# Three loads of batch 3 issued from earlier places in GpSimd's order

## The chip, the cores and the metric

One core of a Trainium2 chip runs the whole kernel. The time is device microseconds of one execution, lower is better.

## The reference

Attention with a feature map, then a two-layer network over the result. For each of 8 batches with 8 heads, 576 positions and 64 features:

```
phi(x) = [exp(p), exp(-p)],  p = x @ w_phi - max|x @ w_phi|      # w_phi: 64 x 128
kv  = phi(k)^T v,   z = sum over positions of phi(k)
x   = (phi(q) kv) / (phi(q) z + 1e-6)                            # 4608 tokens x 512
g   = elu(x @ w_in),   out = g @ w_out                           # w_in: 512 x 2048, w_out: 2048 x 512
```

q, k, v and the weights come in as float32 and are cast to bfloat16 while they are loaded.

## The kernel before

**Tiles.** The attention goes over 16 groups of four heads, n = 0 to 15; batch b is groups 2b and 2b + 1, so batch 3 is groups 6 and 7. The network goes over 9 chunks of 512 tokens; chunk 1 needs the attention of groups 2 and 3 (batch 1). From batch 1 on, `load` (L213) brings the whole of one batch's k, q or v (576 KB as bfloat16) with one DMA that GpSimd issues (L216). The pool `io` has two buffers for each of k, q and v, so batch 3 takes those of batch 1.

**From a load to its use.** k and q are needed transposed. For groups 0 to 3 TensorE transposes them (`t_pe`, L234); from group 4 on a DMA transpose that SyncE issues does it (`t_dma`, L252: L266 for k and for q of groups 4 and 5, two issues at L261 for q from group 6 on). `k_mm` (L294) and `m_mm` (L368 for groups up to 5, L353 from 6 on) are the first uses of kT and qT. v is multiplied on GpSimd by a weight for each position (`v_scale`, L331) ahead of the product with phi(k) (`kv_mm`, L516). The attention's result xp is transposed by SyncE too, into xT of its chunk (`x_dma`, L656) and into the last chunk (L663). SyncE also issues the stores of the output (L716).

**The network.** For each chunk and each of 16 tiles of hidden features: `h_mm` on TensorE (L672), the exponential on ScalarE (L683), the minimum with 1 on GpSimd (`h_min`, L688), the elu on VectorE (L692); then `o_mm` (L700). The first chunk goes in halves of 256 tokens.

**The order.** Each engine takes its instructions in the order in which the program emits them, and waits where an operand or a buffer isn't there. That order is written out by hand in the string ORDER (L18): each letter is a step (a star or a digit behind it chooses a variant or a PSUM bank), and each occurrence of a letter takes the next entry of the step's list. White space in the string means nothing. The letters that the change and the prediction touch:

```
e=(load, k)  f=(load, q)  g=(load, v)       # GpSimd issues; e and f, g begin with parts of batch 0
E=(v_scale)  F=(v_ones)   r=(h_min)         # GpSimd work
n=(t_dma, k) o=(t_dma, q) z=(x_dma) v=(o_store)   # SyncE issues
A=(k_mm) M=(m_mm) p=(h_mm) t=(o_mm)         # TensorE
q=(h_exp)  s=(h_elu)                        # ScalarE, VectorE
```

Of the kernel before, what the change touches and what calls it, by code (L numbers as in the profile page):

```python
# [19 lines left out]
DFFUV*M2NW6XBBP5Q*M0S4TTM2NNEU6j1kEEUV*j0k*OP2QS4TTM1NW6Xl0S2l1Y4ZTTj5km*mY7ZOP6Q*W3XS0TTp7A5Cp2  # L20
qrqrM3NS0TTissBp4qrj7kA0p3p2CsBqql6mrsrM4Nsp7p3BBM0Nqqp6p2DqqrrrA4BensssO*Cp0qY7Z*p3qp1qrsrrssrs
EW6XBl2m*p0p4qM2qrsrP1p5Q*DqES6TNM0NsS2TTTM0NFErsEFY6Zp7qrO*sA0BBA2BU4UVp7qp6CP5Q*qBt4S0Tforrss
p7qp5CTrsqp6qW2XW0p7ttXDqS2TA0ngrsErsrsEp5p6p7qrtTCp2qFqrrBsp3qqrp5u*BsqssrsrsDFp4qp7qrsErsS0TT
S2TTt6ttA0zzU4CoEUVA2CBBtuBBW4W0p7t6vzXXzzzzM2NA4DqBenvzftrsM0NM2Np7qrstA0BBBCDM2Ntu*O*P7Q*Ct5S2
TTtM6S0TTEEFNtM6NEFU3S0ogEUVA6CtW3TTBBDEp1p0p2XW6Xuqrqqp5qp3p4p7p6srsA0nerrfqqrsssqrsBBM2NqO*rr
p5p4p2qrCsqssDrqp1qp7P3Q*qsp6p5rrssErsFqA2BBM0NCEqp4rrssqrsFt7S0TtS2M5TTTNvvzzzzS0oTTtA5CEU2US0t
Vu*BBDFETTwW2XW4Xvt6A0BBCS2Ttttu*S0M4TTA2CDTFt7ttM0NBBA4BBM2NNCEEEgfDFEEztU0UV*A2CDzzp6qBup5qrr
W0xRt4tBp7qEEressoM0M2p6qrtNNW0xp5qsstu*S2M0p7p6TTrsRNqwp4qqrsS2TTyW0xrrssyp5p7qrqrS2TTnnA0CRp6q
vvzossp4qFU2UV*rsrsBBA5CDzvyzzW2xRp7qp4W0xp3p2rsyBBqrqzqS5TA0nCrrREyzzTssswDBBt7ttS3TTM5NEEEtu*
t2W3xRyA0BBS5ToTtttuCM3NM0NS5TTFFt7U3UA5A0tV*CCDBBDwBBW3xttuA2Czzp4qp5qBBW0xEEEfep7qrFFrrgssst6t  # L30
M1NS3TTtp7qRRM0NM3Np5p2nevvqrsyW0xqrrssEp3p7p4tS0oqrqqrrsssU2UVy*zzRyvzzuvS5TTTTp4qrW1xRp3qp5qrr
ssA0CS6TTp2qp4rDqp3W6qErrssxBBp5qrt2S0oA6BnssRByEtA3sttTTyzCDECFFW5xRyzzBBuvt7tM0A4BBM2NNttM0CED
ENU2UV*wS4TTt6W0W2ttA4nu*vzxxBBM0p7W2tFERqNuCDyxt1p5qA2BBgrsM6Np4qp0wqEECrsU6FfUV*M2NwtRy*A5CS2T
Tp7rsrRy*qtS2ovtsrsBBDETTgp4qrW5xRyp0uvp7qqS2TTsW5xp1qrp4rssqrrssA5nzzzzW2xRCp0qrp7p1p4p3qqqrrss
BBqp2qsyzrsErrFt7S0M5NttDFEETTssS0TToA5CM3Ntt2RyA0CBBBBU3UVM5NtzzzuvW3xRDtS5A0nCtFyEW3t7tTTBxRBD
wA5BBS3TTM0u*Ntp2qCW0xtuM5NFEEyzEU3UVM0NS5TovvrsRp7p3qqrsrsA0CTp4qp2p7qqByrrsp6qp3rqBrrssW4xssp2
qrst7A0BBS4Tp6p3p2ttqrqCqrrsssRyTDFEM0NA5BBM3NCtDuvp2qrsp1qrFt7EW3xp0qp2RyrqrzzzzEM3S5TTttsNssW3
xRyA5BBA0BCCwwDEFEEtut2tS3TTDEEU5UttV*Bt3W4S6S0ttxRy*u*TTTTW6xW4Rtt2xS0TTFU6Uy*Vzzp4p1u*qqrrsW5
p0p7qrssxqrp4p3p1p0qqrqRyssRrrW5xRp7tttsqrszy*y*W3xsp1p5qqrrp6p4p3vzzvqrvzzzzu*vRysszp2zqqrqrrsq
p7sqsrssrst1tttu*vt5tttt7ttuvp4p2p5p3qrtp0uvsqrqsrsqrqrssp4qp1p7t5tp6p0p2ttqqrrrsssp3p4qrqsrsuqq  # L40
qp7p1qrrrssrssp5qrqp2p0qp7rsrqrssp4sqrst1tttuqrst7tttt0tttuvu*vp1qp5p2rqrqrsssp4p7qrsqp1p2p0p5qq
rrqsst7tttuqp1p7qp3rsrqsqrst4ttrrrssstvu*vvt0tttt7ttu*tut6vvvtttuv
"""


# [776 lines left out]
```

## Time and profile before

| | us |
|---|---|
| median of 5 runs | 366.55 (363.94 to 369.86) |
| the profiled execution | 363.94 |
| its span, first to last instruction | 362.2 |
| TensorE busy (modelled) | 341.8 (94%) |
| VectorE, ScalarE, GpSimd busy | 270.0, 251.1, 211.6 |
| mean granted TensorE clock | 1.000 |
| issue of k and q of batch 3 on GpSimd, from the span's start | 63.17, 64.00 |
| issue of v of batch 3 | 75.81 |

Times inside the profile count from the span's start. Busy TensorE is modelled, since matmuls overlap; instructions that only issue a DMA do not count as busy. A line of a timeline has the start, the duration, the engine, the line of the kernel, the operation and its tiles, and in brackets how long the engine had been idle and what ended that.

### The profile page before, as it was taken

The numbers are of one execution on the slowest core, as the hardware profiler recorded it, in microseconds if no ns is written. First come the engines' busy times: TensorE is split into PE (matmuls) and PEld (weight loads), VectorE is DVE, ScalarE is ACT, GpSimd is POOL, SyncE is SP. The second block draws the span as 40 slices with busy tenths as digits, with TensorE's granted clock in tenths as the row PEclk, the third lists the DMA queues.
The fourth block names the chain that finished last, engine by engine and source line by source line (L and its number), as shares of the span: only waits on it lengthen the run. The fifth ranks groups of instructions, "written<-read, shape, count | busy, mean of one in ns | idle before, by whom it ended". The sixth has DMA issues, their size and how long they took to land.

```text
span 362.2 us, 9855 instructions
## 1 busy us (share of the span) xinstructions
PE 341.8 (94%) x3912; PEld 188.5 (52%) x3960; DVE 270.0 (75%) x474; ACT 251.1 (69%) x480; POOL 211.6 (58%) x324
## 2 busy tenths in 40 slices
PE   5788899999999999999999999999999999999994
PEld 3676676654455454545465445544555444444442
DVE  5889986977977999779988999998777914543430
ACT  3998989777897599877976987887855405533401
POOL 8754867358917778386877584766836505432400
PEclk9999999999999999999999999999999999999999
DMA  7999998999966974499478894541214221112123
GB/s 113 198 212 158 195 170 148 172 190 123 168 80 101 181 140 97 82 172 176 86 115 152 129 167 67 77 94 32 52 31 91 63 62 29 29 26 62 24 48 76
DMA packets 68479, 39.72 MB, mean 110 GB/s; under 512 B 48336, under 2 KB 62800, under 8 KB 68432
## 3 DMA queue, kind: packets, MB, share of 16 engines
q0 software_dynamic: 15856, 18.35, 32.5%
q1 hardware_dynamic: 52416, 20.56, 32.4%
q8 instruction: 31, 0.51, 0.6%
q10 hardware_dynamic: 160, 0.16, 0.1%
q14 instruction: 16, 0.13, 0.1%
HBM read 36.77 MB, written 9.44 MB: 128 GB/s over the span
## 4 chain that ended last, share of the span: by engine, by line
PE 78%; DVE 9%; ACT 6%; issue 3%; POOL 2%; DMA 1%; ACTq 0%; POOLq 0%; DVEq 0%
PE banks L700 33%; PE banks L672 26%; PE banks L516 5%; PE banks L549 3%; PE banks L476 3%; DVE gT L692 3%; PE banks L294 2%; PE banks L353 2%; ACT EK L305 2%; ACT Eq L500 2%; DVE mq L395 2%; DVE mk L312 2%; PE banks L565 1%; ACT e_sb L683 1%; PE banks L240 1%
## 5 line engine op out<-in xcount | busy, mean ns | idle before, releaser
L688 POOL TENSOR_SCALAR e_sb<-e_sb 128x512 f32<-128x512 f32 (+1 forms) x160 | 89.9, 572 | 89.6 <-ACT e_sb L683 85.4
L700 PE MATMUL banks<-w_out_sb,gT 128*128 128x512 bf16 x549 | 131.1, 379 | 3.5 <-issue 2.7
L672 PE MATMUL banks<-xT,w_in_sb 128*128 128x512 bf16 (+1 forms) x557 | 119.7, 355 | 1.9 <-DVE mq L395 0.9
L692 DVE SCALAR_TENSOR_TENSOR gT<-e_sb,banks 128x512 bf16<-128x512 f32 (+1 forms) x160 | 94.7, 625 | 35.8 <-POOL e_sb L688 35.3
L683 ACT ACTIVATE e_sb<-banks 128x512 f32<-128x512 f32 (+1 forms) x160 | 87.0, 565 | 36.7 <-PE banks L672 31.8
L672 PEld LDWEIGHTS <-w_in_sb 128*128 128x128 bf16 x640 | 58.9, 98 | 57.7 <-issue 1.9
L700 PEld LDWEIGHTS <-gT 128*128 128x128 bf16 x576 | 52.9, 98 | 61.0 <-issue 2.4
L305 ACT ACTIVATE EK<-banks 128x768 bf16<-128x768 f32 x96 | 73.3, 812 | 13.8 <-PE banks L294 8.8
L500 ACT ACTIVATE Eq<-banks 128x768 bf16<-128x768 f32 (+2 forms) x96 | 72.7, 818 | 13.3 <-PE banks L476 7.8
L331 POOL TENSOR_TENSOR vs<-vn,em 128x576 bf16<-128x576 bf16 x64 | 73.1, 1154 | 13.4 <-ACT em L322 12.7
L312 DVE TENSOR_REDUCE mk<-banks 128x6 f32<-128x768 f32 x48 | 45.2, 951 | 5.4 <-PE banks L294 3.1
L710 ACT COPY o_sb<-banks 128x512 f32<-128x512 f32 x21 | 12.4, 590 | 34.5 <-PE banks L700 32.1
L381 DVE TENSOR_REDUCE mx<-banks 128x6 f32<-128x768 f32 (+1 forms) x30 | 30.6, 1036 | 3.4 <-PE banks L353 3.2
L615 POOL TENSOR_TENSOR xj<-xs,recj 128x448 bf16<-128x448 f32 (+1 forms) x23 | 20.5, 893 | 13.2 <-DVE recj L610 13.2
L594 DVE TENSOR_TENSOR xs<-banks,e 128x455 f32<-128x455 f32 (+1 forms) x30 | 18.1, 603 | 9.3 <-PE banks L549 8.2
L516 PE MATMUL banks<-vs,EK 64*128 64x65 bf16 x1152 | 21.9, 192 | 0.0
L516 PEld LDWEIGHTS <-EK 64*128 64x128 bf16 x1152 | 20.6, 96 | 2.0 <-DVE mx L381 0.8
L549 PEld LDWEIGHTS <-Eq 128*128 128x128 bf16 x400 | 15.9, 98 | 6.2 <-issue 0.3
L599 DVE TENSOR_TENSOR xs<-banks,xs 128x455 f32<-128x455 f32 (+1 forms) x30 | 18.3, 610 | 1.1
L294 PE MATMUL banks<-w_sb,kT 64*128 64x128 bf16 x288 | 16.8, 229 | 2.4 <-DVE kT L247 1.8
L710 DVE COPY o_sb<-banks 128x512 f32<-128x512 f32 x15 | 10.3, 684 | 11.1 <-PE banks L700 11.1
L549 PE MATMUL banks<-kv_sb,Eq 128*128 128x65 bf16 x400 | 17.1, 194 | 0.1
(69 smaller groups left out, 250.3 us busy)
## 6 DMA issues: line engine op xcount, KB each, us to landing
out_dram<-o_sb SPq DMA_DIRECT2D x71, 128.0 KB, 2.4
kn<-in_k_dram POOLq DMA_DIRECT2D x7, 576.0 KB, 9.2
qn<-in_q_dram POOLq DMA_DIRECT2D x7, 576.0 KB, 8.7
vn<-in_v_dram POOLq DMA_DIRECT2D x7, 576.0 KB, 7.9
w_in_sb<-in_moe_w_in_dram POOLq DMA_DIRECT2D x2, 1024.0 KB, 19.5
w_out_sb<-in_moe_w_out_dram POOLq DMA_DIRECT2D x1, 2048.0 KB, 15.2
qn<-in_q_dram POOLq DMA_DIRECT2D x2, 288.0 KB, 7.0
vn<-in_v_dram POOLq DMA_DIRECT2D x2, 288.0 KB, 7.8
```

The costliest lines, as they stand in the source:

```text
L305: nc.scalar.activation(EK[:, sg, 6 * c:6 * c + 6, :].rearrange("p (i r) f -> p r i f", r=2), st["pk", n, c], ACT.Exp, scale=1.0 - 2.0 * sg,)
L312: nc.vector.tensor_reduce(mk[:, 6 * c:6 * c + 6].rearrange("p (i r) -> p r i", r=2), st["pk", n, c], axis=AX.X, op=ALU.max, apply_absolute ...
L331: nc.gpsimd.tensor_tensor(get(("vs", n), new_vs)[:, sg, r, 0:D], st["v", n // 2][:, 2 * (n % 2) + pr], st["em", n][:, sg, r].unsqueeze(2). ...
L381: nc.vector.tensor_reduce(mq.rearrange("p (v r) -> p r v", r=2)[:, :, v0:v1], st["pm", n, c][:, :, 0:v1 - v0, :], axis=AX.X, op=ALU.max, a ...
L500: nc.scalar.activation(Eq[:, sg, :, :, p0 * D:p1 * D].rearrange("p h r x -> p r h x"), st["pq", n, c][:, :, 0:(p1 - p0) * P].rearrange("p ...
L516: nc.tensor.matmul(kv[:, hi, pr, sg, :], EK[rows, sg, pr * NS + s, :], vs[rows, sg, pr * NS + s, :], start=(s == 0), stop=(s == NS - 1),)
L549: nc.tensor.matmul(pn[:, sg, v - v0, :], Eq[:, sg, hi, par, i0 * D:(i0 + 2) * D], kv_sb[:, hi, pr, sg, :], start=True, stop=True,)
L672: nc.tensor.matmul(ph, w_in_sb[:, ct, jt * P:(jt + 1) * P], xT_of(ch)[:, ct, h0:h1], start=(ct == 0), stop=(ct == N_CT - 1),)
L683: nc.scalar.activation(e_sb, st["ph", ch, jt, h0], ACT.Exp)
L688: nc.gpsimd.tensor_scalar(e_sb, e_sb, 1.0, 0.0, op0=ALU.min, op1=ALU.max)
L692: nc.vector.scalar_tensor_tensor(gT[:, jt, h0:h1], st["e", ch, jt, h0], -1.0, st["ph", ch, jt, h0], op0=ALU.add, op1=ALU.max,)
L700: nc.tensor.matmul(po, st["gT", ch][:, jt, tt * P:(tt + 1) * P], w_out_sb[:, jt, :], start=(jt == 0), stop=(jt == N_JT - 1),)
```

## The change

Three letters of ORDER move to earlier places; all other letters keep their order. The string's line breaks shift with them, which means nothing, so the diff is shown here without the breaks ("..." is string left out):

```diff
-...S2TA0ngrsErsrsEp5p6p7qrtTCp2qFqrrBsp3qqrp5u*Bsqss...
+...S2TA0ngrsErsrsEep5p6p7qrtTCp2qFqrrfBsp3qqrp5u*Bsqss...
...
-...M2NA4DqBenvzftrsM0NM2Np7qrstA0BBBCDM2N...
+...M2NA4DqBnvztrgsM0NM2Np7qrstA0BBBCDM2N...
...
-...M6NEFU3S0ogEUVA6CtW3TT...
+...M6NEFU3S0oEUVA6CtW3TT...
```

- The k load of batch 3 (letter e) goes from just ahead of the DMA transpose of group 6's k to just behind the second v scaling of group 3. In GpSimd's order it now has 12 instructions fewer ahead of it.
- The q load (f) goes from three steps behind that (behind the transpose of group 6's k, a store and a piece of xT, all SyncE's) to between the minima of two tiles of chunk 0, 8 GpSimd steps earlier.
- The v load (g) goes from between the v scalings of group 4 to just behind the next minimum after the old place of k and q, 7 GpSimd steps earlier.

The order of the loads among themselves stays: v of batch 2, then k, q and v of batch 3, then k of batch 4. In the program's order the k load moves past SyncE's transposes of group 5's q and of seven of the eight attention pieces of groups 2 and 3 (o, z), and past one output tile's store; the q load past the same, the transpose of group 6's k, a second store and the last piece; the v load past the transposes of group 6's q.

More of the change, by code (lines that the diff above doesn't have):

```diff
@@ L22 @@
 EW6XBl2m*p0p4qM2qrsrP1p5Q*DqES6TNM0NsS2TTTM0NFErsEFY6Zp7qrO*sA0BBA2BU4UVp7qp6CP5Q*qBt4S0Tforrss
[L23 to L39, printed above, removed]
@@ L40 @@
-p7sqsrssrst1tttu*vt5tttt7ttuvp4p2p5p3qrtp0uvsqrqsrsqrqrssp4qp1p7t5tp6p0p2ttqqrrrsssp3p4qrqsrsuqq
-qp7p1qrrrssrssp5qrqp2p0qp7rsrqrssp4sqrst1tttuqrst7tttt0tttuvu*vp1qp5p2rqrqrsssp4p7qrsqp1p2p0p5qq
-rrqsst7tttuqp1p7qp3rsrqsqrst4ttrrrssstvu*vvt0tttt7ttu*tut6vvvtttuv
+p7qp5CTrsqp6qW2XW0p7ttXDqS2TA0ngrsErsrsEep5p6p7qrtTCp2qFqrrfBsp3qqrp5u*BsqssrsrsDFp4qp7qrsErsS0T
+TS2TTt6ttA0zzU4CoEUVA2CBBtuBBW4W0p7t6vzXXzzzzM2NA4DqBnvztrgsM0NM2Np7qrstA0BBBCDM2Ntu*O*P7Q*Ct5S2
+TTtM6S0TTEEFNtM6NEFU3S0oEUVA6CtW3TTBBDEp1p0p2XW6Xuqrqqp5qp3p4p7p6srsA0nerrfqqrsssqrsBBM2NqO*rrp5
@@ new lines @@
+p4p2qrCsqssDrqp1qp7P3Q*qsp6p5rrssErsFqA2BBM0NCEqp4rrssqrsFt7S0TtS2M5TTTNvvzzzzS0oTTtA5CEU2US0tV
+u*BBDFETTwW2XW4Xvt6A0BBCS2Ttttu*S0M4TTA2CDTFt7ttM0NBBA4BBM2NNCEEEgfDFEEztU0UV*A2CDzzp6qBup5qrrW0
+xRt4tBp7qEEressoM0M2p6qrtNNW0xp5qsstu*S2M0p7p6TTrsRNqwp4qqrsS2TTyW0xrrssyp5p7qrqrS2TTnnA0CRp6qvv
+zossp4qFU2UV*rsrsBBA5CDzvyzzW2xRp7qp4W0xp3p2rsyBBqrqzqS5TA0nCrrREyzzTssswDBBt7ttS3TTM5NEEEtu*t2
+W3xRyA0BBS5ToTtttuCM3NM0NS5TTFFt7U3UA5A0tV*CCDBBDwBBW3xttuA2Czzp4qp5qBBW0xEEEfep7qrFFrrgssst6tM1
+NS3TTtp7qRRM0NM3Np5p2nevvqrsyW0xqrrssEp3p7p4tS0oqrqqrrsssU2UVy*zzRyvzzuvS5TTTTp4qrW1xRp3qp5qrrss
@@ new lines @@
+A0CS6TTp2qp4rDqp3W6qErrssxBBp5qrt2S0oA6BnssRByEtA3sttTTyzCDECFFW5xRyzzBBuvt7tM0A4BBM2NNttM0CEDEN
+U2UV*wS4TTt6W0W2ttA4nu*vzxxBBM0p7W2tFERqNuCDyxt1p5qA2BBgrsM6Np4qp0wqEECrsU6FfUV*M2NwtRy*A5CS2TT
+p7rsrRy*qtS2ovtsrsBBDETTgp4qrW5xRyp0uvp7qqS2TTsW5xp1qrp4rssqrrssA5nzzzzW2xRCp0qrp7p1p4p3qqqrrssB
+Bqp2qsyzrsErrFt7S0M5NttDFEETTssS0TToA5CM3Ntt2RyA0CBBBBU3UVM5NtzzzuvW3xRDtS5A0nCtFyEW3t7tTTBxRBDw
+A5BBS3TTM0u*Ntp2qCW0xtuM5NFEEyzEU3UVM0NS5TovvrsRp7p3qqrsrsA0CTp4qp2p7qqByrrsp6qp3rqBrrssW4xssp2q
+rst7A0BBS4Tp6p3p2ttqrqCqrrsssRyTDFEM0NA5BBM3NCtDuvp2qrsp1qrFt7EW3xp0qp2RyrqrzzzzEM3S5TTttsNssW3x
@@ L43 @@
+RyA5BBA0BCCwwDEFEEtut2tS3TTDEEU5UttV*Bt3W4S6S0ttxRy*u*TTTTW6xW4Rtt2xS0TTFU6Uy*Vzzp4p1u*qqrrsW5p0
+p7qrssxqrp4p3p1p0qqrqRyssRrrW5xRp7tttsqrszy*y*W3xsp1p5qqrrp6p4p3vzzvqrvzzzzu*vRysszp2zqqrqrrsqp7
+sqsrssrst1tttu*vt5tttt7ttuvp4p2p5p3qrtp0uvsqrqsrsqrqrssp4qp1p7t5tp6p0p2ttqqrrrsssp3p4qrqsrsuqqq
+p7p1qrrrssrssp5qrqp2p0qp7rsrqrssp4sqrst1tttuqrst7tttt0tttuvu*vp1qp5p2rqrqrsssp4p7qrsqp1p2p0p5qqr
+rqsst7tttuqp1p7qp3rsrqsqrst4ttrrrssstvu*vvt0tttt7ttu*tut6vvvtttuv
 """
```

## The prediction

> **What bounds the kernel now.** I read the page's totals first, then the busy time by window around the loads of batch 3, then GpSimd's, SyncE's and TensorE's timelines there, and last how long each transfer took from issue to landing. The totals and the chain that ended last:
>
> ```profile
> PE 341.8 (94%) x3912; PEld 188.5 (52%) x3960; DVE 270.0 (75%) x474; ACT 251.1 (69%) x480; POOL 211.6 (58%) x324
> ...
> PE 78%; DVE 9%; ACT 6%; issue 3%; POOL 2%; DMA 1%; ACTq 0%; POOLq 0%; DVEq 0%
> ```
>
> TensorE is busy for 94% of the span and owns 78% of the chain; GpSimd, whose order changes, has 2% of it. The stretch that the change touches runs from 55 us (the first new place) to 92 us (after the first use of batch 3's q). Columns: window, its length, then busy time and instructions of PE, PEld, DVE, ACT and POOL, the clock, the DMA share and GB/s.
>
> ```profile
> 55.00:92.00 37.00, 35.95 (x482) 21.40 (x485) 28.70 (x49) 29.86 (x60) 23.10 (x41) 1.00 1.03 156
> ```
>
> TensorE idles for 37.00 - 35.95 = 1.05 us of 37, at full clock. No change here can give more than about 1 us against this execution, unless it reaches beyond the stretch. A loss has no such bound: TensorE takes its instructions in order, so each microsecond for which its next operand is late is a microsecond at the end.
>
> **The change part by part: GpSimd.** No instruction is added or removed and no order among the loads changes; three issues move on one engine. This is its timeline (start, duration; in brackets the idle time before and what ended it):
>
> ```profile
> 54.25 1.14 POOL L331 TENSOR_TENSOR vs<-vn,em 128x576 bf16<-128x576 bf16 x1
> 56.21 0.40 POOL L688 TENSOR_SCALAR e_sb<-e_sb 128x256 f32<-128x256 f32 x1 [0.82 <-ACT e_sb L683]
> ...
> 57.18 0.77 POOL L688 TENSOR_SCALAR e_sb<-e_sb 128x256 f32<-128x256 f32 x2 [0.36 <-ACT e_sb L683]
> 58.44 0.77 POOL L688 TENSOR_SCALAR e_sb<-e_sb 128x256 f32<-128x256 f32 x2 [0.49 <-ACT e_sb L683]
> ...
> 63.17 0.83 POOL L216 DMA_DIRECT2D kn<-in_k_dram  x1
> 64.00 0.75 POOL L216 DMA_DIRECT2D qn<-in_q_dram  x1
> 68.36 0.40 POOL L688 TENSOR_SCALAR e_sb<-e_sb 128x256 f32<-128x256 f32 x1 [3.62 <-ACT e_sb L683]
> 71.12 0.40 POOL L688 TENSOR_SCALAR e_sb<-e_sb 128x256 f32<-128x256 f32 x1 [2.35 <-ACT e_sb L683]
> ```
>
> The k load (0.83 us of issue) goes behind the v scaling that ends at 54.25 + 1.14 = 55.39 and ends at 56.22; the next minimum (L688) started at 56.21 after 0.82 us of idling, so it loses 0.01 us. The q load (0.75) goes behind the pair that ends at 57.95 and ends at 58.70; the next pair started at 58.44, so it loses 0.26 us. The elu on VectorE behind that pair comes in a run of four back to back from 58.02 for 1.64 us, and the next elu starts only at 60.17 after a wait of 0.51 us, so the 0.26 us ends there. The v load (0.84, issued at 75.81 before) goes to 68.76, ahead of an idle gap of 2.35 us: nothing. In return the v scaling at 76.68 can start 0.87 us sooner; TensorE reaches its product at 77.97 without a wait, so that gives nothing. GpSimd's sum: 0. If the cover were gone (ScalarE ahead of GpSimd), the first two issues would cost at most 0.83 + 0.75 = 1.6 us.
>
> No load finds its buffer taken. Batch 3 uses batch 1's tiles: TensorE's last transpose from a k tile starts at 31.9 us and from a q tile at 40.1, and the last scaling of batch 1's v is GpSimd's own at 62.08, before 68.76.
>
> **The change part by part: the transfers.** The loads are issued 63.17 - 55.39 = 7.8, 64.00 - 57.95 = 6.0 and 75.81 - 68.76 = 7.0 us sooner. They move past SyncE's transposes, which use the same DMA engines. First the issues of 63 to 65 us with the time to landing, then the queues of 66 to 69 us (packets, MB, share of 16 engines):
>
> ```profile
> kn<-in_k_dram POOLq DMA_DIRECT2D x1, 576.0 KB, 6.8
> qn<-in_q_dram POOLq DMA_DIRECT2D x1, 576.0 KB, 10.6
> ...
> qT<-qn SPq DMA_TRANSPOSE x1, 4.1
> xT<-xp SPq DMA_TRANSPOSE x1, 10.5
> ...
> q0 software_dynamic: 439, 0.50, 106.8%
> q1 hardware_dynamic: 27, 0.06, 5.4%
> ```
>
> The xT transpose, issued at 64.44 just behind the q load, lands at 64.4 + 10.5 = 74.9, right after that load at 64.0 + 10.6 = 74.6; meanwhile the hardware queue moves next to nothing. So the transfers are served in the order of issue, whole loads at a time, and a transpose issued behind a load waits for all of it. The Trainium skill, "DMA: Bandwidth & Descriptors", section "Queues, rings and completion order", says that an engine goes round the queues packet by packet; by that rule the transposes would share the engines with the loads, nothing below would come late, and the sum would be 363.94 + 0. The rows speak for the order of issue, and the sum goes by them.
>
> What now stands behind the loads, in order of issue: qT of group 4 (53.7), **k**, kT of group 5 (55.6), **q**, two xT pieces (58.3, 59.6), qT of group 5 (60.9), two stores, three xT pieces (64.4 to 67.6), **v**, the last xT pieces of chunk 1 (68.9, 70.2). Landings, from rows: qT of group 4 as before at 53.7 + 5.6 = 59.3. A load behind other transfers takes 4.6 us (q after k: 74.6 - 70.0), so k lands at 63.9. A backlog is quick: from 74.6 to 76.9 five xT pieces and the kT of group 6 (72.3 + 4.6) landed, six in 2.3 us, 0.4 each; 0.9 for a full kT or qT is my estimate from that. So kT of group 5 lands at 64.8, q at 69.4, the two xT pieces and qT of group 5 at 69.4 + 0.8 + 0.9 = 71.1. The stores and three xT take 2 us more (73.1), v 4.6 (77.7), the last xT pieces 0.8 (78.5). When TensorE needs them:
>
> ```profile
> 68.07 0.34 PE L368 MATMUL banks<-w_sb,qT 64*128 64x128 bf16 x6
> ...
> 71.35 0.34 PE L294 MATMUL banks<-w_sb,kT 64*128 64x128 bf16 x6
> 71.74 0.34 PE L368 MATMUL banks<-w_sb,qT 64*128 64x128 bf16 x6
> ...
> 80.31 2.75 PE L672 MATMUL banks<-xT,w_in_sb 128*128 128x512 bf16 x12
> ```
>
> Group 4's q at 68.07 (there from 59.3), group 5's k at 71.35 (64.8, was 60.2), group 5's q at 71.74 (71.1, was 60.9 + 4.1 = 65.0), chunk 1's xT at 80.31 (78.5, was 70.2 + 5.9 = 76.1). So the slack at group 5's q falls from 6.7 to 0.6 us and that at chunk 1 from 4.2 to 1.8. What gains is not needed sooner: group 6's kT landed at 76.9 for a use at 95.10, its qT (issued at 78.0, landed at 83.9 behind the v load) for a use at 88.11. The step's cost has two ends: 0, if a load takes 4.6 us; and if k and q each take 6.8 us, k's whole time from issue to landing, the qT lands 2 x 2.2 = 4.4 us later, at 75.5, and TensorE stands for 75.5 - 71.74 = 3.8 us, with the rest of group 5's q work, the output matmuls and chunk 1 queued behind it. I take 0.3 us, near the lower end, since q after k is the very pair that moves. **Sum:** 363.94 us (the profiled execution: 362.2 us of span and 1.7 around it) + 0 + 0.3 = 364.2. The median of the runs is 366.55, 2.6 above that execution, so I put it at 366.8.
>
> **The rivals.** One, on the other side: **group 5's q comes late.** The load and transpose backlog decides as soon as that qT lands after 71.74. For it: only 0.6 us is left; the v load, alone in the queue, took 7.7 us to land where k took 6.8, so loads vary by more than the slack; and the runs spread from 363.94 to 369.86. Against it: the rates of the very same two loads. Price 3.8 us with loads of 6.8 us and 5.6 with loads of 7.7 (2 x 0.9 more): 370.6 to 372.4. Two: **the loads were a hidden brake, and the change frees it.** In other executions the q transposes of group 6 behind the v load may pass 88.11, where the profiled one leaves 4.2 us; the change takes that load away from them. For it: the unexplained 2.6 us between the median and the profiled execution. Against: in the trace nothing waits there. If all of the 2.6 us and the stretch's 1.05 us came back: 366.55 - 3.65 = 362.9. Three: **GpSimd's cover is gone**, and its 1.6 us comes through VectorE's elu to TensorE: 368.2, which no measurement here would tell from no change. That the change doesn't do what it says (a load waits at its new place) I give almost nothing, by the free buffers above.
>
> **How the numbers follow.** No change to be told, with rival three in it: 0.55. Group 5's q late enough for over 1%: 0.32, the higher of the two because the slack shrinks and gains are bounded by 1.05 us. Hidden brake, over 1%: 0.13. A measurement of this kernel tells about 1% from no change (3.7 us). The likeliest case itself spans 364 to 369, by the 1.6 us of rival three and the spread of the runs; the range is drawn out to 372.0 to hold most of the late case, and to 363.3 for part of the other.
>
> **What would show it.** Right: k, q and v issues near 55.4, 58 and 69 us; the minima next to them moved by under 0.3 us; kT of group 5 landing near 65 and its qT near 71; TensorE's first product with that qT with no wait before it; chunk 1's first matmul (L672) near 80.3; 36 us of TensorE work in 55 to 92. Wrong: a wait of TensorE before L368 near 72 or before L672 near 80 (rival one), transposes that land while a load runs (then the order of issue is not the rule), or over 1 us gained within 55 to 92.

## The result, and the profile after

| | before | changed |
|---|---|---|
| median, us (runs) | 364.64 (79) | 368.14 (44) |
| lowest to highest | 363.0 to 369.97 | 365.84 to 373.86 |
| ratio, 95% interval | | 1.0079, 1.0057 to 1.0101 |
| span of the profiled execution | 362.2 | 365.6 |

The change makes the kernel slower by 0.8%, about 2.9 us of 364.64. (The five runs shown before the prediction had a higher median, 366.55; more runs brought it down. The ratios here and below leave out the slow runs, those more than 1.5% above the fastest of the same kernel; the medians of all runs lie 3.5 us apart.) The two profiled executions differ by 3.4 us, and that is what the traces can account for. (The changed kernel's runs spread further: 18 of the 44 lie from 370.44 us up, and no profile was taken of one of these, so what else stops there is open.) The totals and the chain of the page:

```profile
PE 343.2 (94%) x3912; PEld 188.5 (52%) x3960; DVE 270.1 (74%) x474; ACT 250.9 (69%) x480; POOL 211.3 (58%) x324
...
PE 77%; DVE 8%; ACT 6%; issue 3%; DMA 3%; POOL 2%; SPq 0%; DVEq 0%; ACTq 0%; POOLq 0%
```

The new entry is "DMA 3%" (1% before). The same stretch from 55 to 92 us as before shows where the time went:

```profile
55.00:92.00 37.00, 33.80 (x457) 19.98 (x461) 25.00 (x44) 26.26 (x53) 20.26 (x35) 0.95 0.96 139
```

TensorE did 457 matmuls where it had done 482, it idled for 3.2 us in place of 1.05, and its mean granted clock was 0.95: for about a tenth of the stretch it ran at half speed besides. Chunk 1's first matmul (L672) started at 83.72 in place of 80.31: 3.4 us late, the whole difference of the spans. All that follows lies ahead of it.

GpSimd did what was forecast (this execution runs 0.41 us ahead of the other up to here: the v scaling at 53.84 stood at 54.25):

```profile
53.84 1.14 POOL L331 TENSOR_TENSOR vs<-vn,em 128x576 bf16<-128x576 bf16 x1
54.94 0.83 POOL L216 DMA_DIRECT2D kn<-in_k_dram  x1
55.81 0.40 POOL L688 TENSOR_SCALAR e_sb<-e_sb 128x256 f32<-128x256 f32 x1
...
57.52 0.78 POOL L216 DMA_DIRECT2D qn<-in_q_dram  x1
58.33 0.78 POOL L688 TENSOR_SCALAR e_sb<-e_sb 128x256 f32<-128x256 f32 x2
```

The minimum behind k came at 55.81 (56.21 less 0.41: no delay), the pair behind q at 58.33 (58.44 less 0.41 is 58.03: 0.30 late). The transfers did worse. SyncE's timeline (duration is that of the issue alone), and then from the queue view the issues with the time to landing, in order: k, group 5's kT, q, the first xT_last piece, group 5's qT.

```profile
55.12 3.94 SPq L266 DMA_TRANSPOSE kT<-kn  x1
59.11 3.60 SPq L656 DMA_TRANSPOSE xT<-xp  x1
62.77 1.22 SPq L663 DMA_TRANSPOSE xT_last<-xp  x1
64.10 4.63 SPq L266 DMA_TRANSPOSE qT<-qn  x1
```

```profile
kn<-in_k_dram POOLq DMA_DIRECT2D x1, 576.0 KB, 10.7
kT<-kn SPq DMA_TRANSPOSE x1, 14.1
qn<-in_q_dram POOLq DMA_DIRECT2D x1, 576.0 KB, 11.3
xT_last<-xp SPq DMA_TRANSPOSE x1, 7.3
qT<-qn SPq DMA_TRANSPOSE x1, 8.2
```

The q load landed at 57.5 + 11.3 = 68.8, and only then everything that SyncE had issued from 55.1 on: kT at 69.2, the xT_last piece at 62.8 + 7.3 = 70.0, qT at 72.3. Even the kT, whose issue began before that of q, came behind it: its issue took 3.94 us (2.60 before) and ended at 59.06, after the q load's at 58.30. The loads did not shut the transposes out, though. While the loads ran, the two queues moved packets almost one for one, here from 61 to 63.5 us (packets, MB, share of 16 engines):

```profile
q0 software_dynamic: 332, 0.37, 85.6%
q1 hardware_dynamic: 324, 0.08, 26.6%
```

A packet of the loads (q0) is over four times as large as one of SyncE's queue (q1). At 0.37 MB in 332 packets a load of 576 KB is a little over 500 of them. The transpose of group 5's q took some 1100 small ones in the kernel before, by the packets of 63 to 65 us there, just ahead of its landing at 65.0:

```profile
DMA packets 1227, 0.39 MB, mean 194 GB/s; under 512 B 1181, under 2 KB 1181, under 8 KB 1227
```

So one for one, a transpose that starts beside two loads is done only about when both are. That is worked out from these counts; it was not tested by an experiment.

Now the two engines that waited, VectorE first:

```profile
67.41 0.22 DVE L580 RECIPROCAL rec<-den 128x10 f32<-128x10 f32 x1
70.16 0.82 DVE L582 TENSOR_TENSOR xp<-banks,rec 128x640 bf16<-128x640 f32 x1 [2.53 <-DMA xT_last<-xp]
70.90 0.95 DVE L395 TENSOR_REDUCE mq<-banks 128x6 f32<-128x768 f32 x1
```

```profile
67.87 0.34 PE L368 MATMUL banks<-w_sb,qT 64*128 64x128 bf16 x6
...
68.31 1.04 PE L700 MATMUL banks<-w_out_sb,gT 128*128 128x512 bf16 x4
71.03 0.34 PE L368 MATMUL banks<-w_sb,qT 64*128 64x128 bf16 x6 [1.69 <-DVE xp L582]
71.90 0.51 PE L368 MATMUL banks<-w_sb,qT 64*128 64x128 bf16 x6 [0.52 <-DVE mq L395]
72.34 1.03 PE L672 MATMUL banks<-xT,w_in_sb 128*128 128x256 bf16 x4
73.16 1.89 PE L700 MATMUL banks<-w_out_sb,gT 128*128 128x512 bf16 x4
74.99 0.34 PE L294 MATMUL banks<-w_sb,kT 64*128 64x128 bf16 x6
75.17 0.33 PE L368 MATMUL banks<-w_sb,qT 64*128 64x128 bf16 x6
```

VectorE's multiply for group 3 (L582) writes an xp buffer. There are three, and the one that is next had been group 2's, which the held-back xT_last transpose was still reading. So VectorE stood for 2.53 us until that piece landed at 70.03. TensorE's next product for group 4 (L368) was released by that multiply, which reads a PSUM bank, and the one after it by the reduction (L395) that comes behind it in VectorE's order and reads group 4's first product; there TensorE stood for 1.69 and 0.52 us. And then it ran slowly: four output matmuls (L700) at 73.16 took 1.89 us, where a run of four takes 1.03 to 1.04. The windows of busy time and clock say why; the clock is the third number from the right:

```profile
69.00:71.00 2.00, 0.34 (x2) 0.09 (x1) 0.84 (x2) 0.23 (x1) 0.42 (x1) 1.00 1.17 180
71.00:72.00 1.00, 0.45 (x10) 0.30 (x11) 1.00 (x2) 0.00 (x0) 0.00 (x0) 0.74 0.96 175
72.00:73.00 1.00, 1.00 (x10) 0.62 (x10) 1.00 (x3) 0.00 (x0) 0.00 (x0) 0.50 1.15 193
73.00:74.00 1.00, 1.00 (x4) 0.40 (x3) 0.90 (x2) 0.54 (x2) 0.06 (x1) 0.50 1.10 158
74.00:75.00 1.00, 1.00 (x5) 0.17 (x4) 0.63 (x2) 0.55 (x1) 0.92 (x4) 0.55 1.15 244
75.00:76.00 1.00, 0.84 (x15) 0.63 (x16) 1.00 (x2) 0.58 (x1) 1.00 (x2) 1.00 1.38 177
```

After the stop the granted clock was one half until about 74.9. The same stretch before was this:

```profile
68.51 1.04 PE L700 MATMUL banks<-w_out_sb,gT 128*128 128x512 bf16 x4
69.48 0.51 PE L368 MATMUL banks<-w_sb,qT 64*128 64x128 bf16 x12
69.95 0.60 PE L672 MATMUL banks<-xT,w_in_sb 128*128 128x256 bf16 x4
70.39 1.03 PE L700 MATMUL banks<-w_out_sb,gT 128*128 128x512 bf16 x4
71.35 0.34 PE L294 MATMUL banks<-w_sb,kT 64*128 64x128 bf16 x6
```

From the L700 run at 68.31 to group 5's first k product at 74.99 are 6.68 us, before (68.51 to 71.35) 2.84, so 3.84 more. The stops are 2.2 of them. From the chunk 0 matmuls at 72.34 on it took 2.65 us in place of 1.40 (69.95 to 71.35), about 1.25 for the half clock; the other 0.4 lies around the two products. The execution had been 0.2 ahead and made good 0.2 later, which leaves the 3.4. The mean clock was 0.995 or less in 28 of the 44 runs, this one among them, and 0.998 or more in the eight fastest. The Trainium skill, "TensorE: Matmul & The Clock Gate", Part 1, says that the clock halves after an idle window of about 3.4 us; here a stop of 1.7 us, with 0.52 of another right behind it, was enough.

### The profile page after: what moved, and what is told of

It reads as the page before. It is cut to its first block, busy times and chain, and to the rows that moved or that the text cites. A ratio compares the mean times of both kernels' runs of the same rounds, so it can differ in the third digit from the quotient of the medians.

```text
span 365.6 us, 9856 instructions
## 1 busy us (share of the span) xinstructions
PE 343.2 (94%) x3912; PEld 188.5 (52%) x3960; DVE 270.1 (74%) x474; ACT 250.9 (69%) x480; POOL 211.3 (58%) x324
## 4 chain that ended last, share of the span: by engine, by line
PE 77%; DVE 8%; ACT 6%; issue 3%; DMA 3%; POOL 2%; SPq 0%; DVEq 0%; ACTq 0%; POOLq 0%
PE banks L700 32%; PE banks L672 26%; PE banks L516 4%; PE banks L549 3%; PE banks L476 2%; DVE gT L692 2%; PE banks L294 2%; DMA xT_last<-xp 2%; ACT EK L305 2%; PE banks L353 2%; ACT Eq L500 2%; ACT e_sb L683 2%; DVE mk L312 1%; PE banks L240 1%; DVE mq L395 1%
## 5 line engine op out<-in xcount | busy, mean ns | idle before, releaser
L700 PE MATMUL banks<-w_out_sb,gT 128*128 128x512 bf16 x549 | 132.0, 381 | 3.5 <-issue 2.7
L672 PE MATMUL banks<-xT,w_in_sb 128*128 128x512 bf16 (+1 forms) x557 | 120.1, 356 | 1.9 <-DVE mq L395 0.9
L672 PEld LDWEIGHTS <-w_in_sb 128*128 128x128 bf16 x640 | 59.0, 98 | 57.9 <-issue 2.1
L700 PEld LDWEIGHTS <-gT 128*128 128x128 bf16 x576 | 53.0, 98 | 61.5 <-issue 2.9
```

The costliest lines, as they stand in the source:

```text
L672: nc.tensor.matmul(ph, w_in_sb[:, ct, jt * P:(jt + 1) * P], xT_of(ch)[:, ct, h0:h1], start=(ct == 0), stop=(ct == N_CT - 1),)
L700: nc.tensor.matmul(po, st["gT", ch][:, jt, tt * P:(tt + 1) * P], w_out_sb[:, jt, :], start=(jt == 0), stop=(jt == N_JT - 1),)
```

## The experiments

Three theories went in. One: the two loads in a row hold back the transposes, the xp buffer with them, and VectorE's wait stops TensorE. Two, the prediction's own rival: group 5's qT comes late. Three: the issues cost at their new places on GpSimd. Medians below stand beside the kernel before on the same chip: 366.63 (35 runs) for the first four, 364.80 (29) for the next four, 364.29 (23) for the last four. A part of those runs, 18, 14 and 7 of them, lie above 366.5, which widens every ratio's interval.

**Four buffers for xp in the changed kernel.**

```diff
-    xpool = ctx.enter_context(tc.tile_pool(name="xpool", bufs=3))
+    xpool = ctx.enter_context(tc.tile_pool(name="xpool", bufs=4))
```

> The changed kernel with four buffers for xp in place of three. Theory 1 (the two loads in a row hold back the L663 transpose of group 2, which still reads an xp buffer; VectorE's multiply at L582 for group 3 waits 2.5 us for that buffer, TensorE stops and comes back at half clock): the wait before L582 is gone, the stop of 2.2 us at L368 of group 4 is gone, the clock stays 1.0. Group 5's qT still lands near 72, some 1 us after TensorE wants it, so about 1 us is left: 365 to 366.5, between the two kernels. Theory 2 (group 5's qT is what comes late): no change, 367 to 368. Theory 3 (the loads' issues cost at their new places on GpSimd): no change, 367 to 368.

Median 366.39, ratio 1.0027 (0.9983 to 1.0072), three of its 12 runs (370.2, 371.1 and 698 us) not in the ratio; the span of its profile 364.1, the clock 1.0. VectorE's wait before L582 and TensorE's two stops at L368 are gone, as theory one said; theories two and three had expected 367 to 368. (By time alone the case would be weaker: this interval and the changed kernel's, 1.0057 to 1.0101, overlap.) Group 5's qT landed at 64.4 + 9.0 = 73.4 and TensorE reached its product at 73.68, so that was no wait here. But TensorE was itself late by then, through a stop that no theory had:

```profile
65.80 1.06 PE L565 MATMUL banks<-kv_sb,Eq 128*128 128x65 bf16 x29
68.27 0.50 PE L565 MATMUL banks<-kv_sb,Eq 128*128 128x65 bf16 x11 [1.41 <-issue]
```

TensorE stood for 1.41 us in the middle of one step, with no operand missing ("issue"). The instruction queue q8 fits: in the kernel before it moved a packet between 60 and 62 us, here none in those two but one between 65 and 67. First the line of before, then this kernel's:

```profile
q8 instruction: 1, 0.02, 3.9%
```

```profile
q8 instruction: 1, 0.02, 4.1%
```

The page counts 31 such packets, 0.51 MB, for TensorE's 3912 + 3960 = 7872 instructions: 65 bytes each, so q8 is taken here to bring TensorE's code, which the loads then delay like the transposes. That is argued from the times, not shown. The Trainium skill, "Runtime: NRT & Kernel Launch", section "Instruction fetch mechanics", calls the cost of crossing such a block mostly hidden; if this reading is right, behind two loads in a row it was not.

**k and v moved, q at its old place.** The edit is the change without its second letter move, shown against the kernel before.

```diff
-...srsrsEp5p6...   DqBenvzftrsM0...  U3S0ogEUV...
+...srsrsEep5p6...  DqBnvzftrgsM0...  U3S0oEUV...
```

> Only k and v moved, q at its old place. Theory 1: one load of 4.6 us stands ahead of group 5's kT and the first two xT pieces; the L663 piece lands near 65 to 66, before VectorE wants the buffer at 67.6: no wait, no stop, the time of before (364.6, within 0.5). Theory 2: the same, since group 5's qT lands near 67. Theory 3: the issue of k still costs at its new place, half of the loss or more is left: 366 or over.

Median 365.53, ratio 1.0010 (0.9970 to 1.0049). No wait at L582 for a transfer and no stop at L368; a stop of 0.8 us in L565 was left. Theory one's waits are gone as stated, and by the ratio so is the loss, though the median is 0.4 above the range on record; theory three, which expected 366 or over, does not hold. The xT_last piece landed at 67.6, later than the 65 to 66 expected, and VectorE's multiply came at 68.5, so the margin was about 1 us.

**Only q moved.** The edit is the second letter move alone.

```diff
-...FqrrBsp3...   DqBenvzftrsM0...
+...FqrrfBsp3...  DqBenvztrsM0...
```

> Only q moved, k and v at their old places (so q is issued ahead of k). Theory 1: again one load only ahead of the xT pieces; they land near 64 to 66, no wait at L582, the time of before within 0.5. Theory 2: group 5's qT lands near 66, the time of before. Theory 3: the q issue sits between the two pairs of minima as in the changed kernel and costs there: 365.5 or over.

Median 364.53, from 363.77 to 364.89, ratio 0.9960 (0.9922 to 0.9998). So the q issue at the very place that the changed kernel gives it costs nothing, which ends theory three; what costs is k and q in a row. TensorE's stop in L565 was 0.3 us. Here the kT of group 5, with the q issue behind it, landed before that load:

```profile
qn<-in_q_dram POOLq DMA_DIRECT2D x1, 576.0 KB, 7.2
kT<-kn SPq DMA_TRANSPOSE x1, 4.7
xT<-xp SPq DMA_TRANSPOSE x1, 8.4
```

Its issue began at 55.76 and ended at 58.39; q's ran from 58.08 to 58.91 and the load landed at 65.3, the kT at 60.4. In the changed kernel kT's issue ended after q's, and it landed after it. But the order of the issues' ends is no rule: with k and v moved, the issue of group 5's qT ended at 64.69, after the q load's at 64.21, and it landed at 69.0, ahead of that load at 71.6.

**VectorE held up without any late transfer.** The kernel before, with three reductions that nobody reads:

```diff
+        if (n, part) == (3, 1):
+            idle = small.tile([P, 6], BF16, name="idle")
+            for _ in range(3):
+                nc.vector.tensor_reduce(idle, ...6 x 128 of sel..., axis=AX.X, op=ALU.max)
         xp = xpool.tile([P, 6, 2, D], BF16, name="xp")[:, 0:m]
```

> The kernel before, with three added reductions on VectorE (about 0.8 to 0.95 us each, into a tile that nobody reads) just ahead of the L582 multiply for the second half of group 3; the loads stay at their old places. It imitates the wait of 2.5 us without any late transfer. Theory 1: TensorE stops for about 2 us at L368 of group 4, the granted clock falls to one half for about 3.4 us behind it as in the changed kernel, and the time rises by 2 to 4 us: 366.6 to 368.6. Theory 2 and 3: VectorE has slack there, and the time rises by under 1 us.

Median 367.71, from 366.73 to 368.49, ratio 1.0062 (1.0025 to 1.0098). VectorE's and TensorE's lines (L592 is the multiply of L582, moved down by ten lines):

```profile
68.23 2.87 DVE L584 TENSOR_REDUCE idle<-sel 128x6 bf16<-128x768 bf16 x3
71.02 0.81 DVE L592 TENSOR_TENSOR xp<-banks,rec 128x640 bf16<-128x640 f32 x1
```

```profile
71.89 0.34 PE L368 MATMUL banks<-w_sb,qT 64*128 64x128 bf16 x6 [1.88 <-DVE xp L592]
72.75 0.34 PE L368 MATMUL banks<-w_sb,qT 64*128 64x128 bf16 x6 [0.52 <-DVE mq L395]
...
75.58 0.34 PE L368 MATMUL banks<-w_sb,qT 64*128 64x128 bf16 x6 [0.77 <-DMA qT<-qn]
```

2.87 us on VectorE gave 2.4 us of stop at the same two products as in the changed kernel, so VectorE has at most about 0.5 us of slack at that place, and the time rose by the expected amount. In this profile the clock stayed at 1.00 through both stops; in 8 of the 12 runs its mean was 0.995 or less. So the half clock follows such a stop in some executions only. The third stop is group 5's qT, which here was issued at 63.9, beside the k and q loads, and landed behind them: theory two's wait exists in this kernel too. From 67 to 70 us, while it shared the engines with the loads, the packets went one for one again:

```profile
q0 software_dynamic: 433, 0.48, 92.4%
q1 hardware_dynamic: 434, 0.11, 27.6%
```

**k and q together, 1.6 us sooner than before.** Both letters go directly behind the third v scaling of group 3.

```diff
-...rsErsS0TT...    DqBenvzftrsM0...
+...rsEefrsS0TT...  DqBnvztrsM0...
```

> k and q of batch 3 issued one v scaling (1.2 us) sooner than in the kernel before, together, v at its old place. Theory 1 in its wider form (what matters is whether SyncE's transposes are issued ahead of the two loads or behind them): the qT of group 5, issued at 60.9 in the kernel before, now stands behind both loads or just ahead of them, by chance; where it is behind, it lands near 74 to 75, TensorE waits 3 us for it at L368 near 71.7 and the clock falls: a good part of the runs near 368, median 365.5 to 368. GpSimd theory: both issues sit beside v scalings, and nothing changes: 364.6.

Median 365.49, from 363.93 to 366.28, ratio 0.9996 (0.9960 to 1.0032). In its profile group 5's qT was issued behind both loads, it landed at 73.5, and TensorE's only wait for a transfer in the stretch was this:

```profile
PE banks L368 <- DMA qT<-qn: 1.0, 1, 1.0
```

The wait is the expected one; its size is not: 1 us in place of 3, and no half clock. None of the 12 runs was near 368, where the text on record expected a good part.

**k and q together, one minimum later.** The minimum (r) goes ahead of them.

```diff
-...DqBenvzftrsM0...
+...DqrBenvzftsM0...
```

> k and q of batch 3 issued behind the next minimum (near 68.8 in place of 63.2), v at its old place. Theory 1, wider form: group 5's qT and the first xT pieces are always ahead of both loads, so no wait of TensorE for them; the kT of group 6 lands near 77 (wanted at 95) and its qT near 86 (wanted at 88.1): 363 to 364.5, no runs near 368. A theory in which an earlier load is better or all places are alike: 364.6 or more.

Median 364.21, ratio 0.9967 (0.9932 to 1.0001), 12 of 13 runs from 363.99 to 365.47. The one at 367.30 is the profiled one, and it shows the next operand in line: group 6's qT behind these two loads and v's, too late for its use near 88. A clock of one half followed (0.50 from 91 to 93 us), and the span was 365.5 where the kernel before had 362.2. TensorE's wait there:

```profile
PE banks L353 <- DMA qT<-qn: 2.0, 1, 2.0
```

**The changed kernel with four xp buffers and fewer warm-up matmuls**, to move the edges of TensorE's code blocks by 64 instructions.

```diff
-    UNREAD, UNREAD_COLS, UNREAD_BANK = 46, 16, 7
+    UNREAD, UNREAD_COLS, UNREAD_BANK = 14, 16, 7
```

> The changed kernel with four xp buffers, and 14 in place of 46 of the warm-up matmuls at the start whose result nobody reads. With four buffers alone TensorE stood 1.41 us in the middle of L565 near 67 with nothing that it waited for, behind an instruction fetch at 65.5 us. If that is the fetch of the next block of TensorE's instructions, held back by the loads, 32 fewer matmuls (64 instructions) put the block's edge 64 instructions later, some 3 us later in time, and the stop is gone or stands at another line. If the stop comes from L565 itself (an operand), it stays in L565. The start may lose up to 1 us; time 364.5 to 366.

Median 371.45, ratio 1.0051 (0.9995 to 1.0107), with 7 of its 12 runs, from 371.31 up, not in the ratio; the time is well above what was expected, and fewer warm-up matmuls change the start too, so it is not used. The stop in L565 is gone: TensorE's longest "issue" wait after 30 us is 0.3 us, at L700. That agrees with a code fetch as its cause, but does not prove it, since all else moved as well. What its profile adds is theory two at full size, once the xp buffer no longer stops VectorE first:

```profile
PE banks L368 <- DMA qT<-qn: 4.9, 1, 4.9
```

**The two loads kept apart.** k alone one minimum later (q, no longer behind it, is issued at 63.3), and q at its new place with k one minimum later:

```diff
-...FqrrBsp3...   CoEUV...   DqBenvzftrsM0...
+...FqrrBsp3...   CoEfUV...  DqrBenvztsM0...
```

```diff
-...FqrrBsp3...   DqBenvzftrsM0...
+...FqrrfBsp3...  DqrBenvztsM0...
```

> k of batch 3 issued behind the next minimum (near 68.8), q and v at their old places. So one load stands between 63 and 68 in place of two, and the fetch of TensorE's instructions at 60.7 is ahead of it. Theory 1 (wider form: transposes behind two loads in a row come too late): even where group 5's qT falls behind the q load it lands near 69, before 71.7: 363 to 364.5, with no runs near 368. A rival, that the runs near 368 come from elsewhere (start, other batches): about one run in three near 368 as in the kernel before.

> q of batch 3 at the place of the changed kernel (near 58), k behind the next minimum (near 68.8), v at its old place: no two loads of batch 3 in a row. Theory 1: no late transpose, no runs near 368; the instruction fetch of TensorE near 61 stands behind the q load as with q alone moved and may cost 0.3 us: 363.5 to 364.8. The rival: runs near 368 remain.

Medians 364.56 and 364.35, ratios 0.9988 (0.9952 to 1.0024) and 0.9981 (0.9946 to 1.0015). The first expectation said 363 to 364.5 and no run near 368; the median is a little over, and one of the 12 runs came at 367.06. Above 366.5 lie 1 and 0 of the 12 runs of these two, 0 of 12 with only q moved, 3 of 12 with k and v moved; of the kernel before it is 18 of 35 and 7 of 23 beside them. But the two kernels that keep k and q in a row and only shift both have 0 of 12 and 1 of 13 as well. So it is not the row of loads alone that makes those runs of the kernel before; a close race would fit (the issue of group 5's qT ends at 60.91 + 2.20 = 63.1 there, that of the k load begins at 63.17), but that is argued and not shown.

**The kernel before, three more profiles**, to catch one of its runs near 368.

> The kernel before, once more, for a second profile. If it lands near 364: as the first profile. If it lands near 368: theory 1, wider form, expects group 5's qT issued behind the q load of batch 3, landing near 75, and TensorE waiting for it at L368 near 72, with a stretch of half clock behind it.

> The kernel before once more, for a profile of one of its runs near 368. Theory 1, wider form: group 5's qT is issued behind batch 3's k or q load, lands after 72, TensorE waits for it at L368, and where the wait is long the clock halves for 3.4 us. The rival: the time goes elsewhere.

> As the run ahead of it: one more profile of the kernel before, with the same two readings.

364.02, 363.97 and 363.82: none of them was such a run. The third speaks against the close race: there the issue of group 5's qT (62.09 to 63.40) did fall beside the k load's (62.42 to 63.25), and the qT still landed at 68.5, ahead of that load at 70.9 and in time for its use at 71.0. The clocks of the runs tell a part: of the kernel before's 87 runs beside the experiments, all 27 above 367.6 us have a mean clock of 0.995 or less and all others 0.997 or more. So a stretch of half clock belongs to those runs, as in the run at 367.30 above. Which wait comes ahead of it stays open.

## Why the prediction was right, and where its steps failed

**The time: right.** 368.14 lies in 363.3 to 372.0, and a ratio of 1.0079 is within 1%, the likeliest case. The sum under it was not right: it put the cost at 0.3 us, and the profile shows 3.4. That the forecast, 366.8, came within 1.4 us is luck: its base of 366.55 was 1.9 above the median of more runs, which made up for much of the missing cost. From 364.64 the same sum gives 364.9.

**GpSimd's part: right.** 0.30 us at the pair of minima where 0.26 was forecast, nothing behind it; q alone at its new place made nothing slower. Rival three fell with it. No load waited for a buffer.

**The transfers: late as forecast, but not by the rule behind it.** Transposes did land behind the loads. Forecast and measured landings: q 69.4 and 68.8, the first xT_last piece 70.2 and 70.0, group 5's qT 71.1 and 72.3, the last xT piece of chunk 1 78.5 and 78.2. Two missed: k, 63.9 and 65.6, and group 5's kT, 64.8 and 69.2. The prediction took whole loads in the order of issue and set aside the sharing of the engines packet by packet, since by that nothing would come late. The counts above speak for the sharing while the loads ran (324 packets beside 332, 434 beside 433), and transposes of many small packets come late under it too: kT shared with both loads and landed 0.4 us behind the second. The row that the prediction went by (27 packets beside 439, 66 to 69 us before) is as measured; why SyncE's queue stood there is open. The issues of SyncE themselves stretched from 2.6 to 3.9 us and from 2.2 to 4.6.

**The list of who needs what: this step failed.** For each held-back transpose the prediction asked when its output is wanted. It did not ask who wants its input's buffer. The xT_last piece is not wanted before the last chunk, so it was passed over; but until it has read xp, VectorE can't write the next one. With three buffers that came due at 67.6, four microseconds before the qT that was watched. Four buffers took the wait away; a pause of the same length on VectorE, with the loads at their old places, gave the same two stops.

**The price of a stop: too low.** A microsecond late was counted as a microsecond at the end. In the profiled execution 2.2 us of stop cost 3.4, mainly since the clock halved behind it.

**Rival one** named the right queue and the wrong operand. Its wait, group 5's qT, would have come next: it landed at 72.3, and TensorE, undisturbed, would have wanted it near 71.4 (71.74, with this execution 0.2 to 0.4 us ahead). It showed with 0.8, 1.0 and 4.9 us in three of the experiments. Its price of 3.8 us was close to what the other wait cost.

**Rival two**, a hidden brake of the kernel before, was not what the change frees, but the runs of the kernel before above 366.5, nearly absent where the loads stand elsewhere, suggest that it has one. Moving q alone had the lowest ratio with an interval below one, 0.9960, and the tightest runs.

## What to carry to other kernels

When a transfer moves, list for every transfer that it delays both its readers and the next writer of the buffer that it reads; a small ring of buffers makes an output that nobody is waiting for into a stop. Look at a chain of loads by how many run in a row, and compare their packets with those of the transposes beside them: one load ahead of the transposes was free here, two were not. Where TensorE fills 94% of the span, allow each stop of 2 us a half-clock tail before calling it small.

## What the runs showed of the hardware that was not expected

- DMA transposes went one packet for one with the loads beside them: 324 to 332 in 2.5 us of the changed kernel, 434 to 433 in 3 us of the kernel with the pause. Their packets are smaller and more, so the loads landed first: group 5's kT took 14.1 us to land beside two loads, 4.6 before the change. At other times SyncE's queue stood (27 to 439 from 66 to 69 us of the kernel before).
- The issue of a transpose on SyncE took up to 4.63 us in the changed kernel, with two loads ahead (5.33 with four xp buffers), where the 20 later q transposes of the kernel before took 1.27 us in the median.
- Loads seem to delay the fetch of TensorE's code as well, by the reading above: 1.41, 0.8 and 0.3 us of stop in L565 in three kernels.
- The granted clock fell to one half for about 3.4 us (71.5 to 74.9) behind stops of 1.7 and 0.5 us, fell to one half behind one of 2.0 us in another kernel, and stayed full in a third with stops of 1.88 and 0.52 us.
